# Half 1 of the second layer put behind output chunks 4 and 5, and fifteen small loads between the last weight load and the first store

## The chip, the core and the metric

The kernel runs on one core of a Trainium2 chip. The metric is the device time of one launch in microseconds. TensorE (PE) multiplies, VectorE (DVE) and ScalarE (ACT) read and write its accumulators, GpSimd (POOL) does some elementwise work and issues four small transfers, and SyncE (SP) issues all other transfers. Sixteen DMA engines move the data.

## What is computed

Linear attention over 8 batches and 8 heads, then a soft mixture of 8 experts over all 4608 tokens. Everything is float32. The reference, cut:

```
kv = einsum('bhsd,bhse->bhde', k, v)             # 8 x 8 x 576 x 64
out = einsum('bhsd,bhde->bhse', q, kv)
x = (out / sqrt(mean(out*out) + 1e-6) * g_norm)  # to (4608, 512)
logits = x @ phi                                 # 32 slots: 8 experts x 4
d = softmax of logits over the tokens
slot_input = d.T @ x                             # (8, 4, 512)
for e in range(8):
    h = maximum(slot_input[e] @ w1[e], 0)        # 512 -> 1024
    slot_out[e] = h @ w2[e]                      # 1024 -> 512
c = softmax of logits over the slots
return c @ slot_out                              # (4608, 512)
```

The inputs q, k, v, w1, w2 are read once (61.94 MB) and the result is written once (9.44 MB).

## The kernel before

The program is one hand-written order. Every call goes through the class `Order`, which records the operations, works out from the memory cells which earlier operations each has to wait for, and emits them in the recorded order (line 214 is the line where it makes each call, so nearly all rows of the profile carry L214). Each transfer has a semaphore of its own. At the end SP waits for all transfers that nobody else waited for, then for the last store, and clears the semaphores.

First, 36 token tiles are worked through while q, k and v stream in. Then come the experts. `expert_h(e)` is the first layer. `expert_y(e, hf)` is one expert's share of the second layer for one half (256 columns) of the result: 8 matmuls that accumulate over all experts into `pY[:, hf]`. Half 0 and half 1 lie in two PSUM banks. The weights of the last six experts lie by halves: the units 2, 3, 4 of w2 hold their half 0, the units 5, 6, 7 their half 1, two experts to a unit. Units 5 and 6 are one load of 4 MB, unit 7 is the last load of 2 MB. All loads are issued by SP.

When half 0 is summed, `gather(0)` copies it to SBUF, `mix(0)` multiplies it by a selection matrix, and `output(0, k, f)` makes six output chunks: four matmuls each into two PSUM buffers (three in chunk 5), which ACT and DVE copy into the arena. After each chunk of half 0 comes one `fill`: a matmul of zeros into `pY[:, 0]`. Then come `expert_y(2..7, 1)`, `gather(1)`, `mix(1)` and the chunks 6 to 11.

SP stores the chunks in rows given by `OUT_ROWS`: chunks 0 to 2 in seven pieces dealt out by the table `FIRST` over chosen partitions (five by SP, two by POOL, with a small transfer of POOL, `step_over`, ahead of each), chunks 3 to 5 in one store, 6 and 7 in one, 8 to 11 in the last. All of SP's transfers go into one hardware queue, in the order of issue. The part of the main program in question is this:

```
    gather(0)
    mix(0)
    for k, f in chunks:
        output(0, k, f)
    for e in range(2, NE):
        expert_y(e, 1)
    gather(1)
    mix(1)
```

Of the kernel before, what the change touches and what calls it, by code (L numbers as in the profile page):

```python
# [15 lines left out]
NE = 8  # L16
# [43 lines left out]
)  # L60
STEPS = (7, 6)
SHARED = (5, 11)
HEAD = 144
SCRATCH = 1024
WORK = {
# [207 lines left out]
def row_length(row):  # L273
    return sum(UNIT if part is None else UNIT // 2 for _, _, part in row)
# [13 lines left out]
def soft_moe_linear_attention(nc, first_in, kv_in, q0_in, q1_in, kv4_in, kv5_in, t3_in, w_in, out):  # L288
# [4 lines left out]
    banks = nc.psum(8)  # L293
    arena = const.tile([P, HEAD + ARENA], F32, name="arena")
    phi_sb = arena[:, :128].rearrange("p (g w n) -> p g w n", g=2, w=2)
# [5 lines left out]
    def place(at, n):  # L301
        return arena[:, HEAD + at * KB : HEAD + at * KB + n]

    def load_row(at, src):
        nc.sync.dma_start(place(at, src.shape[-1]), src)
# [14 lines left out]
    def homes(kind, u):  # L320
        at = W_AT[kind, u]
        if at is None:
            return [xflat[:, :UNIT]]
        return [place(a, UNIT // len(at)) for a in at]

    def load_w(kind, u, part=None):
        i = [row[0] for row in W_ROWS].index((kind, u, part))
        lo = sum(row_length(row) for row in W_ROWS[:i])
        n = row_length(W_ROWS[i])
        src = w_in[:, lo * P : (lo + n) * P].rearrange("o (p n) -> (o p) n", p=P)  # L330
        t = homes(kind, u)[part or 0]
        if n > t.shape[-1]:
            t = place(W_AT[kind, u][part or 0], n)
        nc.sync.dma_start(t, src)

    def w_block(kind, u, i):
        parts = homes(kind, u)
        n = UNIT // len(parts)
        k, at = divmod(i * 256, n)
        return parts[k][:, at : at + 256]  # L340


    nc.sync.dma_start(arena[:, : HEAD + 2304], first_in)
    load_row(KV_AT[0] + 9, kv_in[0, :, 2304:])
# [19 lines left out]
    ident = const.tile([P, P], F32, name="ident")  # L364
# [321 lines left out]
    def fill(n, cols=256, home=None):  # L686

        if not n:
            return
        t = home if home is not None else ps.tile([P, 2, 512], F32, tag="o", name="fill", bufs=2)[:, 1]  # L690
        for i in range(n):
            nc.tensor.matmul(
                t[:, :cols].rearrange("p (a n) -> p a n", n=256),
                lhsT=zeros[:, :P],
                rhs=zeros.unsqueeze(1).to_broadcast([P, cols // 256, 256]),
                start=True,
                stop=True,
            )
# [166 lines left out]
    pY = ps.tile([P, 2, 512], F32, tag="y", name="pY", bufs=1)  # L865

    def w2_unit(e, hf):
        first = NE - LATE
        if e < first:
            return e, 8 * hf  # L870
        return first + hf * LATE // 2 + (e - first) // 2, 8 * (e % 2)

    def expert_h(e):
        ph = ps.tile([P, 2, 512], F32, tag="m", name=f"ph{e}")[:, 0, :256]
        for c in range(4):
            for j in range(4):
                nc.tensor.matmul(
                    ph[32 * j : 32 * j + 32],
                    lhsT=sTe[:, (4 * e + c) * NS : (4 * e + c + 1) * NS],
                    rhs=w_block("w1", e, 4 * c + j),  # L880
                    start=c == 0,
                    stop=c == 3,
                )
        h = wk.tile([P, 256], F32, tag="part", name=f"h{e}", bufs=3)
        nc.scalar.activation(h, ph, AF.Relu, scale=rs)

        x = xts[(NT - 1 - e // 2) % NX].rearrange("p j n -> p (j n)")
        hTs[e] = x[:, e % 2 * 256 : e % 2 * 256 + 256].rearrange("p (c n) -> p c n", n=NS)
        nc.vector.transpose(out=hTs[e].rearrange("p c n -> p (c n)"), in_=h)

    def expert_y(e, hf, cs=range(8)):
        u, at = w2_unit(e, hf)
        for c in cs:
            j = c % 4
            nc.tensor.matmul(
                pY[32 * j : 32 * j + 32, hf, :256],
                lhsT=hTs[e][:, c],
                rhs=w_block("w2", u, at + c),
                start=e == 0 and c < 4,
                stop=e == NE - 1 and c >= 4,  # L900
            )
# [7 lines left out]
    def halves(name, srcs):  # L909
        t = [wk.tile([P, 2, P], F32, tag="part", name=f"{name}_{f}", bufs=3)[:, f] for f in range(2)]  # L910
        nc.vector.tensor_copy(out=t[0], in_=srcs[0])
        nc.scalar.copy(t[1], srcs[1])
        return t
# [4 lines left out]
    def mix(hf):  # L918
        pz = [ps.tile([P, 2, 512], F32, tag="m", name=f"pz{hf}_{f}")[:, 0, :P] for f in range(2)]
        for f in range(2):  # L920
            nc.tensor.matmul(pz[f], lhsT=sel.rearrange("p a n -> p (a n)"), rhs=ys[hf][f], start=True, stop=True)
        zs[hf] = halves(f"z{hf}", pz)

    def step_over(n):
        ends = [x[:n, : 2 * w].rearrange("p (c n) -> p c n", c=2)[:, :, :4] for x, w in ((stepped, 8), (first_in, 64))]
        nc.gpsimd.dma_start(*ends)
# [3 lines left out]
    def store_first(n):  # L930
        at = 0
        for engine, p0, step, m, a, c, k0, k1 in FIRST:
            size = (k1 - k0) * CHUNK
            if k1 == n + 1:
                src = place(OUT_AT[k0], size)[p0 : p0 + step * (m - 1) + 1 : step]
                dst = out[:, at : at + m * size]
                if c > 1:
                    src = src.rearrange("p (c n) -> p c n", c=c)
                dst = dst.rearrange("o (b a n) -> (o a) b n", a=a, n=size // c)
                getattr(nc, engine).dma_start(dst, src)  # L940
                if engine == "gpsimd" and steps:
                    step_over(steps.pop())
            at += m * size

    def output(hf, k, f):
        z = zs[hf]
        n = (hf * NCH + k) * 2 + f
        at = OUT_AT[n]
        st = place(at, 4 * CT * NS).rearrange("p (a n) -> p a n", a=4)
        shared = n in SHARED  # L950
        for v in range(2):
            fourth = hf == 1 and (2 * n + v) % 4 == 3
            apart = shared and v == 1
            pots = [
                ps.tile([P, 2, 512], F32, tag="y" if y else "m", name=f"po{hf}_{k}_{f}_{v}_{i}", bufs=1 if y else None)
                for i, y in enumerate((False, fourth) if apart else (fourth,))
            ]
            for u in range(2):
                lo = 32 * (2 * v + u)
                po = pots[u if apart else 0]  # L960
                nc.tensor.matmul(
                    po[:, 0 if apart else u, : CT * NS].rearrange("p (g x) -> p g x", g=2),
                    lhsT=z[f][lo : lo + 32],
                    rhs=cT[k][lo : lo + 32],
                    start=True,
                    stop=True,
                )
            if apart:
                nc.vector.tensor_copy(out=st[:, 2], in_=pots[0][:, 0, : CT * NS])
                nc.scalar.copy(st[:, 3], pots[1][:, 0, : CT * NS])  # L970
            elif v == 0:
                nc.scalar.copy(st[:, 0:2], pots[0][:, :, : CT * NS])
            else:
                nc.vector.tensor_copy(out=st[:, 2:4], in_=pots[0][:, :, : CT * NS])
        if hf == 0:
            fill(1, home=pY[:, 0], cols=512)
        if n <= OUT_ROWS[0][-1]:
            store_first(n)
        for row in OUT_ROWS[1:]:
            if row[-1] == n:  # L980
                lo, m = row[0] * 4 * CT * NS, len(row) * 4 * CT * NS
                nc.sync.dma_start(
                    out[:, lo * P : (lo + m) * P].rearrange("o (p n) -> (o p) n", p=P), place(OUT_AT[row[0]], m)
                )
# [11 lines left out]
    for e in range(3, NE):  # L996
        expert_h(e)
        if e == 3:
            load_w("w2", 5)
        if e == 4:  # L1000
            combine(2)
        if e == 5:
            load_w("w2", 7)
    expert_y(2, 0)
    expert_y(3, 0)
    expert_y(0, 1)
# [3 lines left out]
    chunks = [(k, f) for k in range(NCH) for f in range(2)]  # L1010
    gather(0)
    mix(0)
    for k, f in chunks:
        output(0, k, f)
    for e in range(2, NE):
        expert_y(e, 1)
    gather(1)
    mix(1)
    for k, f in chunks:
# [3 lines left out]
def build_program():  # L1023
# [3 lines left out]
    shapes = {  # L1027
        "first": (P, HEAD + 2304), "kv": (4, P, TOK), "q0": (P, TOK), "q1": (P, 2048),
        "kv4": (P, 2560 + TOK), "kv5": (P, 2 * TOK), "t3": (P, 3 * TOK),
# [69 lines left out]
```

## Time and profile before

| | |
|---|---|
| time, median of 2 runs | 171.77 us (171.74 to 171.80) |
| time of the profiled execution | 171.88 us |
| its span, first to last instruction | 170.6 us |
| busy: PE, DVE, ACT, POOL | 150.1, 86.8, 89.0, 59.6 us |
| moved by DMA | 71.65 MB, 420 GB/s over the span |
| last PE work; last store issued | about 160.5 us; 161.13 us |

The span is the time between the first and the last instruction of the program; the launch takes 1.28 us more in the profiled execution. The busy time of PE is modelled and says how long work was in its pipeline. The DMA share of a stretch is the time of the packets that began in it over the time of the sixteen engines, so in a stretch of 1 us it is a rough number (a packet of the last store takes nearly that long), and it can be over 1.

### The profile page before, as it was taken

Reading aid. Unit: us, or ns where it says so; the run is one execution under the profiler, and the core shown is the slowest. Engines: PE = TensorE matmul, PEld = TensorE weight load, DVE = VectorE, ACT = ScalarE, POOL = GpSimd, SP = SyncE. Lnnn points to the kernel's source line nnn. Section 1 sums busy time; section 2 is a strip of 40 time slices with the busy share of each in tenths; the row PEclk is TensorE's granted clock in tenths of the full one; section 3 lists DMA queues with packets and bytes.
Section 4 is the critical chain, followed back from the end, with each engine's and each line's share of the span. In section 5 each row is a group of like instructions: output and inputs, shape, how many; then the busy total and the mean of one; then the engine's idle time right before and its main releaser. Section 6 shows DMA issues by size and latency. Waiting matters only on the chain.

```text
span 170.6 us, 4246 instructions
## 1 busy us (share of the span) xinstructions
PE 150.1 (88%) x1838; PEld 105.1 (62%) x1838; DVE 86.8 (51%) x185; ACT 89.0 (52%) x230; POOL 59.6 (35%) x73
## 2 busy tenths in 40 slices
PE   7887897989999899999899998989999989999500
PEld 3466776979678888896697674345566533455200
DVE  1122156283677266762946698823888136306600
ACT  3127576796975887859759864202223034406600
POOL 7000708648357745377382679400000004000000
PEclk9999999999999999999999999999999999999985
DMA  5999999999999999999999999999999999999997
GB/s 181 422 432 419 444 414 441 474 416 444 458 427 408 445 441 415 434 392 459 423 442 407 444 403 417 440 446 407 430 426 446 440 442 392 421 419 429 419 421 323
DMA packets 4365, 71.65 MB, mean 420 GB/s; under 512 B 790, under 2 KB 790, under 8 KB 922
## 3 DMA queue, kind: packets, MB, share of 16 engines
q1 hardware_dynamic: 3994, 71.18, 97.8%
q8 instruction: 14, 0.23, 0.5%
q0 software_dynamic: 352, 0.20, 0.4%
q14 instruction: 5, 0.04, 0.1%
HBM read 61.94 MB, written 9.44 MB: 418 GB/s over the span
## 4 chain that ended last, share of the span: by engine, by line
PE 50%; DMA 24%; ACT 12%; DVE 6%; SPq 2%; issue 1%
PE psum L214 50%; DMA arena<-in_kv_dram 13%; DMA arena<-in_w_dram 10%; ACT bd L214 3%; ACT sq L214 3%; ACT xall L214 2%; SPq L214 2%; DVE logits L214 1%; DVE ms L214 1%; ACT part L214 1%; ACT arena L214 1%; ACT d L214 1%; DVE part L214 1%; ACT r L214 1%; DVE acc L214 1%
## 5 line engine op out<-in xcount | busy, mean ns | idle before, releaser
L214 PE MATMUL psum<-bd,arena 128*128 128x192 f32 (+1 forms) x320 | 56.1, 335 | 1.9 <-ACT bd L214 1.5
L214 PEld LDWEIGHTS psum<-bd,arena 128*128 128x128 f32 (+1 forms) x320 | 45.4, 179 | 8.6 <-ACT bd L214 2.8
L214 DVE TENSOR_REDUCE ms<-sq 128x16 f32<-128x1024 f32 (+1 forms) x19 | 22.1, 1162 | 32.7 <-ACT sq L214 32.5
L214 POOL TENSOR_TENSOR part<-part,r 128x512 f32<-128x512 f32 x17 | 17.8, 1048 | 49.5 <-DVE r L214 49.5
L214 POOL TENSOR_TENSOR xall<-xall,r 128x512 f32<-128x512 f32 x34 | 34.7, 1042 | 0.0
L214 ACT ACTIVATE sq<-psum 128x512 f32<-128x512 f32 x36 | 21.5, 598 | 12.8 <-PE psum L214 12.7
L214 PE MATMUL psum<-arena 128*64 128x64 f32 (+1 forms) x640 | 21.7, 226 | 3.2 <-DMA arena<-in_kv_dram 2.6
L214 PEld LDWEIGHTS psum<-arena 128*64 128x64 f32 (+1 forms) x640 | 19.0, 137 | 8.6 <-DMA arena<-in_kv_dram 3.8
L214 ACT COPY xall<-psum 128x512 f32<-128x512 f32 x34 | 20.7, 608 | 0.0
L214 ACT COPY part<-psum 128x256 f32<-128x256 f32 (+1 forms) x38 | 13.7, 359 | 11.8 <-DVE part L214 10.6
L214 DVE TENSOR_REDUCE logits<-part 128x64 f32<-128x512 f32 (+1 forms) x18 | 17.8, 989 | 0.0
L214 PE MATMUL psum<-arena,xall 128*32 128x256 f32 x256 | 14.8, 380 | 0.2 <-DMA arena<-in_w_dram 0.2
L214 PE MATMUL psum<-logits,part 32*128 32x384 f32 x96 | 13.6, 527 | 0.6 <-ACT arena L214 0.4
L214 DVE COPY arena<-psum 128x768 f32<-128x768 f32 (+1 forms) x12 | 10.5, 890 | 5.8 <-PE psum L214 5.7
L214 ACT COPY arena<-psum 128x768 f32<-128x768 f32 (+1 forms) x14 | 10.2, 753 | 5.6 <-PE psum L214 5.6
L214 POOL DMA_DIRECT2D out_dram<-arena x2 | 1.2, 590 | 33.6 <-DVE arena L214 33.6
L214 PE MATMUL psum<-arena,sq 128*32 128x256 f32 x224 | 12.7, 379 | 0.2 <-DVE sq L214 0.2
L214 PEld LDWEIGHTS psum<-arena,xall 128*32 128x32 f32 x256 | 8.3, 110 | 5.9 <-issue 0.9
L214 PE MATMUL psum<-xall,d 128*32 128x258 f32 x144 | 10.8, 390 | 0.8 <-ACT d L214 0.8
L214 ACT COPY bd<-psum 64x128 f32<-64x128 f32 (+1 forms) x32 | 9.9, 308 | 1.6 <-PE psum L214 1.4
L214 PEld LDWEIGHTS psum<-arena,sq 128*32 128x32 f32 x224 | 7.2, 110 | 5.1 <-DVE sq L214 0.5
L214 PEld LDWEIGHTS psum<-logits,part 32*128 32x128 f32 x96 | 6.0, 183 | 5.4 <-ACT arena L214 3.3
(80 smaller groups left out, 126.4 us busy)
## 6 DMA issues: line engine op xcount, KB each, us to landing
arena<-in_w_dram SPq DMA_DIRECT2D x4, 4096.0 KB, 23.6
arena<-in_w_dram SPq DMA_DIRECT2D x4, 2048.0 KB, 20.3
arena<-in_t_dram SPq DMA_DIRECT2D x1, 6912.0 KB, 36.1
arena<-in_w_dram SPq DMA_DIRECT2D x2, 3072.0 KB, 22.7
arena<-in_kv_dram SPq DMA_DIRECT2D x2, 2304.0 KB, 23.6
arena<-in_kv_dram SPq DMA_DIRECT2D x1, 4608.0 KB, 43.0
arena<-in_kv_dram SPq DMA_DIRECT2D x1, 3584.0 KB, 32.6
arena<-in_kv_dram SPq DMA_DIRECT2D x3, 1152.0 KB, 13.5
```

The source lines that it names most:

```text
L214: inst = getattr(engine, method)(*args, **kwargs)
```

## The change

There are two edits. The first takes the fill out of `output` and puts it behind the chunks 0 to 3 only. Behind chunk 4 come `expert_y(2, 1)` and `expert_y(3, 1)`, behind chunk 5 the four others. The second edit issues fifteen small loads on SP, of 15, 14, ... 1 rows of 16 bytes each, into parts of `ident` (the identity matrix, which nothing reads any more). They stand behind the load of unit 7 and ahead of the first store.

```
+BEHIND = {4: (2, 3), 5: (4, 5, 6, 7)}
...
+    marks = ident[:16, :64]
...
-        if hf == 0:
-            fill(1, home=pY[:, 0], cols=512)
...
+    for n in range(15, 0, -1):
+        nc.sync.dma_start(marks[:n, 4 * n : 4 * n + 4], first_in[:n, 4 * n : 4 * n + 4])
     expert_y(2, 0)
     expert_y(3, 0)
     expert_y(0, 1)
...
-    for k, f in chunks:
+    for n, (k, f) in enumerate(chunks):
         output(0, k, f)
-    for e in range(2, NE):
-        expert_y(e, 1)
+        for e in BEHIND.get(n, ()):
+            expert_y(e, 1)
+        if n < 4:
+            fill(1, home=pY[:, 0], cols=512)
     gather(1)
     mix(1)
```

On PE, before, from the matmuls of chunk 3 to those of chunk 6 (`zeros` is a fill, `logits,part` the four matmuls of a chunk, `arena,xall` the second layer, `part,sel` the mix):

```order
L214 MATMUL psum<-logits,part0 128x384 x4
L214 MATMUL psum<-zeros 128x512
L214 MATMUL psum<-logits,part2 128x384 x4
L214 MATMUL psum<-zeros 128x512
L214 MATMUL psum<-logits,part0 128x384 x4
L214 MATMUL psum<-zeros 128x512
L214 MATMUL psum<-arena,xall 32x256 x48
L214 MATMUL psum<-part1,sel 128x128
L214 MATMUL psum<-part2,sel 128x128
L214 MATMUL psum<-logits,part0 128x384 x4
```

The 48 matmuls of half 1 stand in one piece behind the last fill. The same stretch of PE in the change:

```order
L215 MATMUL psum<-logits,part0 128x384 x4
L215 MATMUL psum<-zeros 128x512
L215 MATMUL psum<-logits,part2 128x384 x4
L215 MATMUL psum<-arena,xall 32x256 x16
L215 MATMUL psum<-logits,part0 128x384 x4
L215 MATMUL psum<-arena,xall 32x256 x32
L215 MATMUL psum<-part1,sel 128x128
L215 MATMUL psum<-part2,sel 128x128
L215 MATMUL psum<-logits,part0 128x384 x4
```

Two fills are gone, and 16 of the 48 matmuls have moved ahead of chunk 5.

On SP, in the change, from the load of units 5 and 6 to the store of chunks 3 to 5, with the thirteen rows of 14 to 2 rows left out here (`ident<-in_first_dram` is a small load):

```order
L215 DMA arena<-in_w_dram 128x8192
L215 DMA arena<-in_w_dram 128x4096
L215 DMA ident<-in_first_dram 15x4
...
L215 DMA ident<-in_first_dram 1x4
L215 DMA out_0_dram<-arena 5x6x1536
L215 DMA out_0_dram<-arena 3x2x512
L215 DMA out_0_dram<-arena 32x3072
L215 DMA out_0_dram<-arena 64x4608
L215 DMA out_0_dram<-arena 64x1536
L215 DMA out_0_dram<-arena 128x4608
```

Before, the first store (5x6x1536) stood directly behind the last load (128x4096).

## Rows read from the trace of the kernel before

**Rows 1.** The page: span, busy time, DMA share in 40 slices, bytes.

```profile
span 170.6 us, 4246 instructions
...
PE 150.1 (88%) x1838; PEld 105.1 (62%) x1838; DVE 86.8 (51%) x185; ACT 89.0 (52%) x230; POOL 59.6 (35%) x73
...
DMA  5999999999999999999999999999999999999997
...
DMA packets 4365, 71.65 MB, mean 420 GB/s; under 512 B 790, under 2 KB 790, under 8 KB 922
```

**Rows 2.** By stretch: us, busy (x) by engine, PEclk, DMA share, GB/s.

```profile
2.00:169.00 167.00, 149.18 (x1837) 104.71 (x1835) 86.04 (x182) 87.73 (x230) 58.71 (x65) 0.99 1.00 427
...
152.00:157.00 5.00, 4.26 (x46) 2.40 (x40) 2.41 (x4) 2.14 (x5) 0.00 (x0) 1.00 1.04 433
157.00:158.00 1.00, 1.00 (x12) 0.56 (x8) 0.89 (x2) 1.00 (x2) 0.00 (x0) 1.00 0.86 369
158.00:161.50 3.50, 2.27 (x16) 0.94 (x14) 2.46 (x4) 2.37 (x4) 0.00 (x0) 1.00 0.97 414
161.50:162.50 1.00, 0.00 (x0) 0.00 (x0) 0.00 (x0) 0.00 (x0) 0.00 (x0) 1.00 0.98 418
...
169.50:170.60 1.10, 0.00 (x0) 0.00 (x0) 0.00 (x0) 0.00 (x0) 0.00 (x0) 0.50 0.01 0
```

**Rows 3.** Timeline of SP's transfers: start us, us of the issue, what.

```profile
122.82 0.33 SPq L214 DMA_DIRECT2D arena<-in_w_dram  x1
...
126.27 0.33 SPq L214 DMA_DIRECT2D arena<-in_w_dram  x1
...
140.31 0.95 SPq L214 DMA_DIRECT2D out_dram<-arena  x1
...
147.74 0.36 SPq L214 DMA_DIRECT2D out_dram<-arena  x1
...
156.99 0.34 SPq L214 DMA_DIRECT2D out_dram<-arena  x1
...
161.13 0.33 SPq L214 DMA_DIRECT2D out_dram<-arena  x1
```

**Rows 4.** DMA issues from 122 us on: KB, us from issue to landing.

```profile
arena<-in_w_dram SPq DMA_DIRECT2D x1, 4096.0 KB, 21.8
...
arena<-in_w_dram SPq DMA_DIRECT2D x1, 2048.0 KB, 23.2
...
out_dram<-arena SPq DMA_DIRECT2D x1, 3072.0 KB, 9.4
out_dram<-arena SPq DMA_DIRECT2D x1, 2304.0 KB, 11.9
...
out_dram<-arena SPq DMA_DIRECT2D x1, 180.0 KB
```

**Rows 5.** Timeline of PE, chunk 4 to the mix of half 1.

```profile
144.25 0.93 PE L214 MATMUL psum<-logits,part 32*128 32x384 f32 x8
...
145.43 1.76 PE L214 MATMUL psum<-logits,part 32*128 32x384 f32 x8
147.13 0.39 PE L214 MATMUL psum<-zeros 128*128 128x512 bf16 x1
147.45 5.39 PE L214 MATMUL psum<-arena,xall 128*32 128x256 f32 x96
```

**Rows 6.** DMA queues from 140 to 171 us: packets, MB, share of 16 engines.

```profile
q0 software_dynamic: 320, 0.20, 2.0%
```

**Rows 7.** The page: queue that fetches instructions, its share of the whole span.

```profile
q14 instruction: 5, 0.04, 0.1%
```

**Rows 8.** SP's issues early on, and the chain's piece of one load.

```profile
3.84 0.44 SPq L214 DMA_DIRECT2D arena<-in_kv_dram  x1
...
10.39 1.28 SPq L214 DMA_DIRECT2D arena<-in_kv_dram  x3
...
3.84 22.89 DMA arena<-in_kv_dram
```

## The prediction

> **What bounds the kernel now.** I read the page first: PE looks like the bound with 88% busy, but the DMA line shows a nine in every slice but the first and the last [rows 1]. So I asked for the DMA share by stretch. From 2 to 169 us the sixteen engines are taken up to a share of 1.00, at 427 GB/s [rows 2]. The reader is to see that 71.65 MB at 427 GB/s are 167.8 us, and that with some 2 us before the stream runs and about 1 us for the last bytes to be confirmed this is the span of 170.6 us. The kernel is a stream of transfers from end to end. PE matters only where it lets that stream run dry.
>
> Where could it? PE and the copies supply the stores, and the timeline of SP tells when each was issued: chunks 0 to 2 from 140.31, chunks 3 to 5 at 147.74, 6 and 7 at 156.99, 8 to 11 at 161.13 [rows 3]. The store of chunks 3 to 5 took 11.9 us to land although its 2304 KB move in 5.5 us at 427 GB/s: it stood behind other work in the queue. The last store took 9.4 us for 3072 KB, which move in 7.4 us [rows 4]. Its issue (0.33 us) and the last confirmation (share 0.01 from 169.5 on, landing at 161.13 + 9.4 = 170.5) leave less than 1 us in which it waited for its turn. So the queue gets short toward the end, and the windows show it: share 0.86 from 157 to 158, 0.97 from 158 to 161.5, 0.98 in the microsecond after the last issue [rows 2]. The engines without work there add up to 0.14 + 0.03 x 3.5 + 0.02 = 0.27 us, as a mean over sixteen. That is all that an earlier PE can give back on average.
>
> **The change part by part.** *PE.* Before, chunk 4 starts at 144.25, chunk 5 at 145.43, and the 48 matmuls of half 1 run from 147.45 to 152.84 [rows 5]. Chunk 4 takes 0.93 us when its PSUM buffers are free; chunk 5 takes 1.76 us because its buffers have to be emptied first. In the change chunk 4 ends at 145.2, and 16 matmuls of the second layer follow (5.39 / 3 = 1.8 us, with the 0.2 to 0.3 us that lie between pieces: to 147.2). By then the buffers are empty, so chunk 5 takes about 0.95 us (to 148.2), and the last 32 take 3.6 us (to 152.0). Half 1 is ready some 0.9 us earlier (0.4 if chunk 5 still needs most of its 1.76, 1.2 if no gaps remain), and so are the stores at 156.99 and 161.13. The two fills need no price of their own: they lay in these 8.6 us.
>
> The weights allow it. Units 5 and 6 land at 122.82 + 21.8 = 144.6, before 145.2; unit 7 lands at 126.27 + 23.2 = 149.5, and expert 6 asks for it at about 150.2 [rows 3, 4]. If either is late, PE waits, and the cost is a part of the 0.9 us.
>
> What moves the other way is the store of chunks 3 to 5. Chunk 5 ends at 148.2 instead of 147.2, so that store is issued 1.0 us later, at 148.8. Its cover is the 11.9 - 5.5 = 6.4 us for which it waited or was being confirmed; without that cover it would cost the 1.0 us.
>
> What is it worth? The end belongs to the DMA engine that ends last. An engine that had no work at 157.5 comes out earlier by as much; one that was never idle does not. The mean idle time is 0.27 us, and idle time is most likely with engines that were ahead. So I count 0 for the end (bounds: a gain of 0.27 us, and nothing).
>
> *The fifteen small loads, on SP.* A regular load costs SP 0.33 us, the store of 5 x 6 rows 0.95 us [rows 3]. Fifteen of them are 5 to 14.3 us. They follow the load of unit 7 (issued by 126.6), so SP is free again between 131.6 and 140.9; the first store is issued at 140.31. In the worst case it goes out 0.6 us later, behind a load that lands only at 149.5. Hidden.
>
> *On the DMA engines.* From 140 to 171 us POOL's queue took 2.0% of 16 x 31 us, 9.9 us [rows 6]. The 0.19 MB in 32 packets of its two stores are 7.3 us at 427/16 = 26.7 GB/s, so 288 small packets took 2.6 us, some 9 ns each. The fifteen loads have 120 rows, and I count one completion beside each row: 240 packets, 2.2 us of engine time. Spread evenly that is 0.14 us; if row i always goes to engine i, the first gets 30 packets, 0.27 us, and the fifteenth two; all on one engine, 2.2 us. The store of 5 x 6 rows has no landing time in its row, as the view gives one only for sixteen completions [rows 4], so a transfer of few rows runs on few engines, and the stairs are the likely case. I take 0.14 us, the engine that ends last being any of them.
>
> The Trainium skill (DMA: Bandwidth & Descriptors, "Why a DMA increments its semaphore by 16 and not by 1") says that such a transfer takes the lowest-numbered engines; by it the first engine pays the 0.27 us and the last none. Nothing in the rows names the engines.
>
> *Instructions.* SP has some 23 more (15 transfers, 8 double waits at the end, which run while the last store moves). If they bring one more instruction fetch, that costs 0.1% of 16 x 170.6 us over 5 packets, 0.55 us on one engine [rows 7]. I take 0 and keep 0.55 for the range.
>
> **The sum.** Span 170.6 - 0 + 0.14 + 0 = 170.75 us. The profiled execution took 171.88, 1.28 over its span and 0.11 over the median of the runs. So 170.75 + 1.28 - 0.11 = 171.9 us: no change that can be told from the 171.77 now.
>
> **The rivals.**
>
> *A: the end follows PE.* The dips at 157.5 and after 161 speak for it. If the engines that idle were also the last ones, the end would come 0.27 us earlier, less 0.1 for the small loads: 171.6. The whole 0.9 us (171.0) would need all engines to have stood still for 0.9 us, and the shares of 0.86 to 0.98 exclude that.
>
> *B: SP's queue blocks (the other side).* The fifteen loads stand in the queue behind two weight loads and can't complete before unit 7, at 149.5. If the queue holds only a few transfers, SP stands still with a small load in hand, and the first store waits behind it. This decides once the first store goes out after about 146, when the first engines run out of weights. At worst it goes out at 149.5 instead of 140.31; 9.44 MB at 427 GB/s are 22.1 us, so with 1 us each for issue and confirmation the span is 173.6 and the time 174.8, and up to 176 if the uneven dealing of the first stores no longer fits. Against it: at 10.39 SP issued three loads in 1.28 us, no slower than others, while the load of 3.84 (landed 26.73) and one more were under way [rows 8]. That shows five or more in the queue, not fifteen.
>
> *C: each small load pays its own latency.* The three issues in 1.28 us speak against it, since none waited for one before [rows 8]. A price from rows: the issue-to-queue time of the last store, under 1 us, fifteen times in a row on the first engine would be up to 15 us, and the time 172 to 186.
>
> The same page gives a transfer of GpSimd's about 2.0 us fixed ("Anatomy of one DMA") and advises to join small transfers into one ("Rules for kernel authors"); fifteen such fixed costs one after another would be an estimated 30 us. The back-to-back issues of this trace disagree with reading it as a queue of latencies.
>
> *D: the small packets or a fetch fall on the engine that ends last.* 0.55 to 2.2 us there: 172.4 to 174.0.
>
> **How the numbers follow.** Forecast (171.65 to 172.3) 0.63; A 0.20; B 0.06, half of it over 2%; C 0.02; D 0.09. 2% is 3.4 us, about what a measurement can tell from no change. None of the cases gains that, since the bytes stay and the engines idle for 0.27 us: faster 0.01. Slower takes half of B and C, with a little of D: 0.05. The range 171.2 to 172.7 holds the forecast, A, and the nearer part of D.
>
> **What would show it.** Right: the stretch from 152 to 168 still at a share of 1.00 with no dip at 157.5; the last store issued near 160.2 but landing at about 170.5, so its row says over 10 us; the store of chunks 3 to 5 issued near 148.8. SP through with the small loads before 140.9, and the first store at 140.3 to 140.9. Wrong: a gap between the small loads on SP, or a first store after 146 (B); an end that comes earlier by as much as the last issue (A); 240 packets with a share of over 0.2% (C, D).

## The result, and the profile after

The changed kernel takes 173.82 us (173.66 to 173.98, 2 runs) against 171.77 before: 1.0116 of the time, with an interval of 1.0099 to 1.0132. That is 2.05 us slower, under the 2% line, but outside the range of 171.2 to 172.7. The profiled execution spans 172.3 us, against 170.6 [rows 1]. In one of the runs below, that with one load in place of fifteen, one execution of ten took 193.42 us, in a slow state of the chip, and is left out of its median.

SP's timeline of the changed kernel answers to [rows 3] (start us, us of the issue, what):

```profile
126.55 5.40 SPq L215 DMA_DIRECT2D ident<-in_first_dram  x15
...
140.21 0.91 SPq L215 DMA_DIRECT2D out_dram<-arena  x1
...
149.04 0.38 SPq L215 DMA_DIRECT2D out_dram<-arena  x1
...
155.56 0.36 SPq L215 DMA_DIRECT2D out_dram<-arena  x1
...
159.70 0.33 SPq L215 DMA_DIRECT2D out_dram<-arena  x1
```

SP issued the fifteen small loads in 5.40 us, long before the first store, which went out at 140.21. The last store was issued 1.43 us earlier than before. So far everything is ahead of time. But the row of the last store (KB, us from issue to landing) and the stretches say where the time went:

```profile
out_dram<-arena SPq DMA_DIRECT2D x1, 3072.0 KB, 12.6
```

```profile
146.00:152.00 6.00, 5.59 (x93) 2.67 (x86) 0.98 (x3) 1.39 (x3) 0.00 (x0) 1.00 1.03 360
152.00:168.00 16.00, 6.52 (x52) 3.44 (x51) 5.45 (x7) 5.30 (x9) 0.00 (x0) 0.81 1.01 430
...
169.00:170.00 1.00, 0.00 (x0) 0.00 (x0) 0.00 (x0) 0.00 (x0) 0.00 (x0) 0.50 0.91 393
170.00:171.00 1.00, 0.00 (x0) 0.00 (x0) 0.00 (x0) 0.00 (x0) 0.00 (x0) 0.50 0.23 98
171.00:172.40 1.40, 0.00 (x0) 0.00 (x0) 0.00 (x0) 0.00 (x0) 0.00 (x0) 0.50 0.04 18
```

The last two columns are the DMA share and GB/s. From 146 to 152 us, where the queue goes from the last weights over the small loads to the first stores, the engines count as fully taken (1.03) and yet move 360 GB/s. Behind 152 the rate is 430 again. At the end few engines are left: a packet of the last store has 24 KB, so 98 GB/s from 170 to 171 is about four of them, and 18 GB/s after that is one. The last store needs 12.6 us to land instead of 9.4 [rows 4], and lands at 159.70 + 12.6 = 172.3.

### The profile page after: what moved, and what is told of

Read it like the earlier page. It is cut to its first block, busy times and chain, and to the rows that moved or that the text cites. A ratio compares the mean times of both kernels' runs of the same rounds, so it can differ in the third digit from the quotient of the medians.

```text
span 172.3 us, 4264 instructions
## 1 busy us (share of the span) xinstructions
PE 149.2 (87%) x1836; PEld 104.3 (61%) x1836; DVE 86.8 (50%) x185; ACT 88.9 (52%) x230; POOL 59.6 (35%) x73
## 2 busy tenths in 40 slices
DMA packets 4605, 71.65 MB, mean 416 GB/s; under 512 B 1030, under 2 KB 1030, under 8 KB 1162
## 4 chain that ended last, share of the span: by engine, by line
PE 49%; DMA 23%; ACT 12%; DVE 6%; SPq 2%; issue 1%
PE psum L215 49%; DMA arena<-in_kv_dram 13%; DMA arena<-in_w_dram 10%; ACT bd L215 3%; ACT sq L215 3%; ACT xall L215 2%; SPq L215 2%; DVE logits L215 1%; DVE ms L215 1%; ACT part L215 1%; ACT arena L215 1%; ACT d L215 1%; DVE part L215 1%; ACT r L215 1%; DVE acc L215 1%
## 5 line engine op out<-in xcount | busy, mean ns | idle before, releaser
L215 ACT ACTIVATE sq<-psum 128x512 f32<-128x512 f32 x36 | 21.5, 598 | 12.6 <-PE psum L215 12.4
L215 PE MATMUL psum<-logits,part 32*128 32x384 f32 x96 | 12.7, 527 | 0.6 <-ACT arena L215 0.4
L215 PEld LDWEIGHTS psum<-logits,part 32*128 32x128 f32 x96 | 5.5, 183 | 5.2 <-ACT arena L215 2.9
```

The costliest lines, as they stand in the source:

```text
L215: inst = getattr(engine, method)(*args, **kwargs)
```

## The experiments

All ran beside the kernel before, which took 171.84 us in the first four and 171.94 in the other four. Two theories stood at the start. S: the small loads hold their DMA engines far longer than their packets show. P: the new order of PE, which issues one store later and two earlier, makes the loss.

### The new order of PE without the small loads

Against the changed kernel, cut:

```
...
-    for n in range(15, 0, -1):
-        nc.sync.dma_start(marks[:n, 4 * n : 4 * n + 4], first_in[:n, 4 * n : 4 * n + 4])
...
```

> The change without the fifteen small loads: half 1 stands behind the chunks 4 and 5, SP's queue is that of before. Theory S (the small loads hold their DMA engines): in the stretch from 146 to 152 us the changed kernel moved 360 GB/s where before moved 426, a loss of 66 x 6 us = 0.40 MB, or 0.93 us of the whole stream; over 120 rows that is about 0.12 us of an engine each, 1.9 us for an engine that has fifteen. Without them the time is that of before or a little less: 171.3 to 171.9 us, 425 GB/s in that stretch, last store issued near 159.7 and landed at about 170.3. Theory P (the new order of PE costs the time: the store of chunks 3 to 5 goes out at 149.0 instead of 147.7, or the earlier last store runs into others): about 173.8, with the rate of 360 GB/s.

Measured: 171.89 us, ratio 1.0 (0.999 to 1.0009). The last store's issue in the timeline, its row among the transfers, and three stretches:

```profile
159.83 0.33 SPq L215 DMA_DIRECT2D out_dram<-arena  x1
```

```profile
out_dram<-arena SPq DMA_DIRECT2D x1, 3072.0 KB, 10.7
```

```profile
146.00:152.00 6.00, 5.59 (x93) 2.66 (x85) 1.11 (x3) 1.30 (x4) 0.00 (x0) 1.00 1.01 420
...
157.00:158.00 1.00, 1.00 (x12) 0.42 (x7) 0.85 (x2) 0.69 (x2) 0.00 (x0) 1.00 0.92 393
...
169.00:170.00 1.00, 0.00 (x0) 0.00 (x0) 0.00 (x0) 0.00 (x0) 0.00 (x0) 0.50 0.23 98
```

The store is issued 1.3 us earlier than before and lands at 159.83 + 10.7 = 170.5, as before (161.13 + 9.4). P falls. PE's new order is worth nothing that shows in the time: the interval leaves it 0.2 us either way.

### The small loads without the new order of PE

Against the kernel before, cut:

```
...
         if e == 5:
             load_w("w2", 7)
+    for n in range(15, 0, -1):
+        nc.sync.dma_start(marks[:n, 4 * n : 4 * n + 4], first_in[:n, 4 * n : 4 * n + 4])
...
```

> Before with the fifteen small loads alone, PE's order as before. Theory S: the loss of the changed kernel stays, less what the earlier PE gave back: 173.5 to 174.5 us, about 360 GB/s from 146 to 152. Theory P: 171.8 to 172.0 (their 240 packets at 9 ns).

Measured: 173.76 us, 1.0105 (1.009 to 1.0121). From 146 to 152 us:

```profile
146.00:152.00 6.00, 6.00 (x93) 3.38 (x93) 0.84 (x2) 1.34 (x3) 0.00 (x0) 1.00 1.03 361
```

The low rate and the loss (1.92 us) are there without the first edit. The change in time is that of the small loads.

### One load of the same sort in place of fifteen

Against the changed kernel, cut:

```
...
-    for n in range(15, 0, -1):
-        nc.sync.dma_start(marks[:n, 4 * n : 4 * n + 4], first_in[:n, 4 * n : 4 * n + 4])
+    ends = [x[:16, :128].rearrange("p (c n) -> p c n", n=8)[:, :, :4] for x in (ident, first_in)]
+    nc.sync.dma_start(*ends)
...
```

> The change with one small load of 16 rows x 16 pieces of 16 bytes in the place of the fifteen: 256 data packets, 16 on each engine if a row goes to an engine, but one completion instead of fifteen. If each small data packet holds its engine for 0.12 us (theory S, data): every engine loses 16 x 0.12 = 1.9 us, 173.5 to 173.9. If what holds the engine is a transfer's completion (theory S, completions): one completion, 171.4 to 172.0.

Measured: 172.05 us, 1.001 (1.0 to 1.0019). The stretch:

```profile
146.00:152.00 6.00, 5.59 (x90) 2.73 (x83) 0.85 (x2) 1.45 (x3) 0.00 (x0) 1.00 1.01 408
```

More pieces of 16 bytes (256 instead of 120) cost 0.2 us (by the interval 0 to 0.3) instead of 2. So it is not the pieces that cost. It is the number of transfers, each of which has a completion of its own.

### The fifteen loads spread over the kernel

Against the changed kernel, one of the places, cut (`small_load()` issues the next of the loads of 15 to 1 rows):

```
...
+        small_load()
         nc.sync.dma_start(t, src)
...
```

> The change with the same fifteen loads of 15 to 1 rows, each issued by SP directly ahead of one of the fifteen last big loads, instead of all together behind the last one (they write unused columns of other tiles, since the identity matrix is still in use then). If a small load holds its engine by itself (packet or descriptor work): the same 0.12 us each are lost, only earlier: 173 to 174. If only the pile at one place costs, because a completion has to wait for the data before it and no big packet stands behind it to fill the time: 171.3 to 172.0.

Measured: 172.03 us, 1.0011 (1.0 to 1.0022), with 419 GB/s from 146 to 152:

```profile
146.00:152.00 6.00, 5.59 (x93) 2.68 (x86) 1.06 (x3) 1.31 (x3) 0.00 (x0) 1.00 1.01 419
```

The same fifteen transfers, with a big one behind each, cost about 0.2 us (0 to 0.4). In these runs they are dear only when they follow one another.

### The pile ahead of the last weight load

Against the changed kernel, cut (the fifteen behind the load are gone):

```
...
         if e == 5:
+            for n in range(15, 0, -1):
+                nc.sync.dma_start(marks[:n, 4 * n : 4 * n + 4], first_in[:n, 4 * n : 4 * n + 4])
             load_w("w2", 7)
-    for n in range(15, 0, -1):
-        nc.sync.dma_start(marks[:n, 4 * n : 4 * n + 4], first_in[:n, 4 * n : 4 * n + 4])
...
```

> The change with the same fifteen loads in one pile, but ahead of the last weight load (unit 7) instead of behind it, so that 2 MB of weights follow them in the queue and not the stores. Theory pile (completions of the small loads follow one another on an engine at a fixed pace, and two next to each other have no data between them that could move meanwhile): as bad as the change, 173.3 to 174.1 us, and the weights land later by the same. Theory turn (the loss belongs to the place where the queue turns from reading to writing memory): 171.8 to 172.1.

Measured: 173.45 us, 1.0086 (1.0071 to 1.0101). The hole moves with the pile:

```profile
140.00:146.00 6.00, 6.00 (x51) 2.30 (x51) 3.87 (x5) 3.23 (x5) 1.72 (x3) 1.00 0.97 358
146.00:152.00 6.00, 5.11 (x88) 2.46 (x84) 0.93 (x2) 1.34 (x3) 0.00 (x0) 1.00 1.00 418
```

So the loss does not belong to the turn from loads to stores. It is the pile. The weights landed later, as expected, and PE waited 0.89 us for them. The loss in time is 1.5 us here and 1.9 to 2.05 with the pile behind the load; where the difference went was not tried.

### Fifteen and five loads on every engine

Against the changed kernel, cut; with five the loop is `range(5, 0, -1)`:

```
...
     for n in range(15, 0, -1):
-        nc.sync.dma_start(marks[:n, 4 * n : 4 * n + 4], first_in[:n, 4 * n : 4 * n + 4])
+        nc.sync.dma_start(marks[:16, 4 * n : 4 * n + 4], first_in[:16, 4 * n : 4 * n + 4])
...
```

> The change with fifteen loads of 16 rows each instead of 15 to 1 rows: each of the sixteen engines gets fifteen, none gets fewer. The changed kernel's loss of about 15 us of engine time over 120 rows, and one row for nothing (the spread loads cost 0.2 us in all), give by estimate some 0.18 us a row, less 0.5 us that an engine has covered. Theory pile: every engine loses 15 x 0.18 - 0.5 = 2.2 us, the end moves from 171.9 to 174.1 (more than the change, whose last engines had fewer small loads). Theory once (an engine stalls once where a pile stands, whatever its height): about 0.9 us, 172.8.

> The same with five loads of 16 rows. Theory pile: 5 x 0.18 - 0.5 = 0.4 us, 172.3. Theory once: 172.8. If there is no cover of 0.5 us: 0.9 us, 172.8, which only the slope to the fifteen tells from once.

Measured: 174.40 us with fifteen, 1.0149 (1.0133 to 1.0166); 172.33 with five, 1.0023 (1.0014 to 1.0033). The stretch with fifteen, then with five:

```profile
146.00:152.00 6.00, 5.59 (x95) 2.62 (x85) 1.12 (x3) 1.30 (x4) 0.00 (x0) 1.00 1.03 283
```

```profile
146.00:152.00 6.00, 5.59 (x93) 2.61 (x86) 0.98 (x3) 1.33 (x3) 0.00 (x0) 1.00 1.01 396
```

Ten loads more on every engine cost 174.40 - 172.33 = 2.07 us, so each costs its engine 0.21 us. Five cost 0.39 us over the kernel before and not 1.04: about 0.65 us, or three loads, are covered. "Once" falls, since five and fifteen differ. The rate points the same way: against the 420 GB/s without small loads, fifteen lose 137 GB/s over 6 us, 0.82 MB or 1.9 us of the stream, and five lose 0.3 us. That two measured heights lie on a line with an offset is by construction; a third was not run.

The two traces have the time of every engine's completion, too, and they bear the line out. With fifteen, the last small load completes on an engine 3.29 us after its share of the last weight load, as a mean over the sixteen engines: 0.22 us for each load. With five it is 1.18 us, 0.24 for each. Of both, about 0.8 us do not come back in the time (3.29 - 2.46 and 1.18 - 0.39), near the cover of 0.65 us that the line gives.

### The same fifteen with 2 KB in a row

Against the changed kernel, cut:

```
...
+    free = place(108, 12 * KB)
     for n in range(15, 0, -1):
-        nc.sync.dma_start(marks[:n, 4 * n : 4 * n + 4], first_in[:n, 4 * n : 4 * n + 4])
+        at, lo = 512 * (n % 6), 32 * (n // 6)
+        nc.sync.dma_start(free[lo : lo + 16, at : at + 512], first_in[:16, :512])
...
```

> Fifteen loads of 16 rows again, but with 2048 bytes in a row instead of 16 (0.49 MB in all, 1.15 us of the stream at 427 GB/s; they write a stretch of the arena that is free until chunk 6). If an engine is held by the pace of completions and can move data meanwhile, the 2 KB are free: the time of the fifteen loads of 16 bytes, 174.1. If packet and completion add up: 175.2.

Measured: 176.07 us, 1.0245 (1.0222 to 1.0269), 1.67 us more than with 16 bytes. The row of the last weight load with 16 bytes, the same with 2 KB, and the stretch with 2 KB:

```profile
arena<-in_w_dram SPq DMA_DIRECT2D x1, 2048.0 KB, 23.0
```

```profile
arena<-in_w_dram SPq DMA_DIRECT2D x1, 2048.0 KB, 24.5
```

```profile
146.00:152.00 6.00, 4.88 (x84) 2.33 (x80) 0.72 (x2) 1.18 (x2) 0.00 (x0) 1.00 1.06 301
```

The 2 KB are not free: the time grows by their 1.15 us of the stream and 0.5 us more. Here the last weights also landed 1.2 us later than with 16 bytes (issued at 126.27 and 24.5 us on the way, against 126.57 and 23.0), and PE waited 1.11 us for them, so the sum is not a clean one. The expectation that the 2 KB move for nothing while the completions are outstanding fails by the 1.67 us.

## Why the prediction was wrong

**The bound: right.** It is a stream of transfers from end to end, with PE of no account: the order of PE alone gives 171.89 us.

**PE's part: right in kind and in worth, its steps a little short.** In the changed kernel the matmuls of half 1 end 1.4 us earlier, where 0.9 was forecast and 1.2 was the most; the gaps between pieces that I added were not there. In the timeline of PE, chunk 4 to the end of half 1 (before: [rows 5]):

```profile
144.16 0.93 PE L215 MATMUL psum<-logits,part 32*128 32x384 f32 x8
145.01 1.93 PE L215 MATMUL psum<-arena,xall 128*32 128x256 f32 x32
146.88 0.93 PE L215 MATMUL psum<-logits,part 32*128 32x384 f32 x8
147.74 3.67 PE L215 MATMUL psum<-arena,xall 128*32 128x256 f32 x64
```

Chunk 5 took 0.93 us instead of 1.76, as worked out. The store of chunks 3 to 5 went out at 149.04 (148.8 forecast), hidden. Without the small loads the dip to 0.86 at 157.5 is a share of 0.92, and the end does not move: rival A is out, and so is the fear that the later store costs.

**SP: right.** 5.40 us for fifteen issues lie in the 5 to 14.3 that were given, and the first store went out at 140.21: nothing blocked (rival B).

**Instructions: right.** The page of the changed kernel still counts 14 and 5 packets in the two queues of instructions, as before.

**The small loads on the DMA engines: this is the step that failed.** I priced a small load by the time of its packets, 9 ns each, and got 0.14 us as a mean and 0.27 for the engine with fifteen. By the even loads each costs its engine 0.21 us behind the first three: fifteen cost 2.46 us, not 0.27, and the change as a whole lost 2.05 where the sum had 0.14. The count of 240 packets was right (the page has 4605, before 4365), and so was the division of POOL's 2.0% of the queue time: in the changed kernel, too, nearly all of them are booked with 9 ns. But the quantity was the wrong one. In the pile the packets of the small loads begin in trains 12 ns apart, and their completions come some 0.2 us apart. The wait is booked elsewhere: with fifteen on every engine, the packets that began from 146 to 152 us took 28.6 us more in all than packets of their sizes took before, 1.8 us for each engine (those of 12 KB 0.94 us as a mean instead of 0.46). What the rows gave was a floor, and I took it for the price. For the same reason the sign that was to show C or D stayed silent: 240 packets at 9 ns are 0.08% of the engines' time, under the 0.2%.

The upper bound that I set against it (2.2 us, all packets on one engine) came close to the number by luck, for a reason that isn't the true one: the 173.82 us lie in rival D, which had a chance of 0.09, but no single engine had all the packets (the load of 15 rows reports from fifteen). Rival C was nearer in kind, a wait for each small load, but at 1 us each and not 0.21. I had put it aside because SP issued three loads without waiting [rows 8]. That shows SP's side of the queue. It says nothing of how fast the engines complete what stands in it.

The Trainium skill (DMA: Bandwidth & Descriptors, "Queues, rings and completion order") says that the increment of a semaphore is a strongly ordered write, which lands only after all earlier writes of that DMA engine. With the runs this fits: 256 pieces with one completion cost 0.2 us, fifteen completions in a row cost 2, and fifteen with a big transfer behind each 0.2. The completions 0.22 us apart are measured; that this order of the writes is what takes the 0.22 us is argued and not shown. The advice to join small transfers on the same page of the Trainium skill ("Rules for kernel authors") agrees with the runs: joined, they cost 0.2 us instead of 2.0.

Why 2.05 us, when the rate from 146 to 152 us says that the stream as a whole lost only 0.93? The stairs load the engines unevenly, and the end belongs to those that end last. The completions of the last store show it. In the run with the new order of PE alone, the last three of the sixteen engines report between 170.38 and 170.51 us. In the changed kernel thirteen have reported by 171.13, and three come only at 172.08 to 172.27; the mean is 0.96 us later, the last 1.76. So the mean over sixteen engines, which I took, is too low also where the price is right. With fifteen loads on every engine the mean is 2.18 us later and the last 2.46. That the three late ones are those with the most small loads fits the stairs; no row names the engines.

**No version beats both.** The order of PE alone is even with the kernel before. The stores could be dealt out anew, since three engines end about 1 us behind the others; that was not tried.

## What to carry to other kernels

In this kernel, which streams from end to end, a tiny transfer cost by its place: between big ones next to nothing, in a pile 0.2 us of each of its engines behind the first three. Join such transfers into one with many pieces, or spread them out. Work that PE does earlier brings nothing when the transfers set the end; look first at how far the DMA rate falls in any stretch. And the time of its packets alone is not the price of a transfer.

## What was not expected of the hardware

- A share of the DMA engines of 1.03 can go with 360 or 283 GB/s: the wait behind a pile is booked as longer packets of other transfers (28.6 us in all with fifteen on every engine), so only the rate beside the share shows the hole.
- Fifteen transfers that follow one another on an engine cost 2.5 us with 16 bytes in a row and 4.1 us with 2 KB; 256 pieces of 16 bytes in one transfer cost 0.2.
- SP issued the fifteen small transfers of the changed kernel behind two loads without a pause, 0.36 us each. In the runs with sixteen rows in each of fifteen and with the pile ahead of the last load, one issue of the fifteen took 1.1 to 1.4 us instead of about 0.3 to 0.4; why was not looked into.
